# A list of kernel steps for five engines, laid out anew

## The chip, the cores and the metric

The kernel runs on one core of one Trainium2 chip. The metric is the device time of one execution in microseconds (us), the median of several. A profile of one further execution shows when each engine worked. The engines are TensorE (PE in the profile, its weight loads PEld), VectorE (DVE), ScalarE (ACT), GpSimd (POOL) and SyncE (SP), which issues nearly all of the DMA transfers.

## The reference

Two stages. The first is a gated linear attention with a stabilised exponential gate (an mLSTM cell) over 4 batches, 8 heads, 768 tokens and a head size of 40. The second is a feed-forward network (ffn) with a leaky activation whose slope, `alpha`, is given for each hidden unit; it takes all heads of a token as a row of 320.

```python
for t in range(S):
    m_new = np.maximum(f_gate[:, :, t] + m, i_gate[:, :, t])
    f_stab = np.exp(f_gate[:, :, t] + m - m_new)
    i_stab = np.exp(i_gate[:, :, t] - m_new)
    m = m_new
    C = f_stab[:, :, None, None] * C + i_stab[:, :, None, None] * np.einsum('bhd,bhe->bhde', vt, kt)
    n = f_stab[:, :, None] * n + i_stab[:, :, None] * kt
    h_tilde = np.einsum('bhde,bhe->bhd', C, qt)
    nq = np.einsum('bhd,bhd->bh', n, qt)[:, :, None]
    denom = np.maximum(np.abs(nq), 1.0)
    o = 1.0 / (1.0 + np.exp(-o_gate[:, :, t]))
    y[:, :, t] = o * h_tilde / denom
x = y.transpose(0, 2, 1, 3).reshape(B * S, H * D)   # 3072 x 320
h = x @ w_in                                        # w_in 320 x 2048
g = np.maximum(h, 0.0) + alpha * np.minimum(h, 0.0)
out = g @ w_out                                     # w_out 2048 x 320
```

Inputs and output are float32, except `w_in` and `w_out`, which arrive as float64 and are made into float32 on the chip by integer operations.

## The kernel before

**Tiles and stages.** A chunk is 128 tokens of one batch; there are 24. Within a chunk the attention is a product of scores with values under a decay matrix, plus a product with the state left by the chunks before. Two chunks make a group of 256 tokens, and the ffn works on one group at a time: 12 groups, each in 8 steps up (two blocks of 128 hidden units) and 8 steps down. For accuracy each float32 operand of the ffn is split into a high and a low part in a faster format, so that one step up has 16 products of 256 columns and one step down 12 products of 320 columns. The attention of chunks 0 to 5 (`NDIR = 6`) uses plain float32 products; from chunk 6 on it uses parts in bfloat16.

**The list.** The first two groups of the ffn, the attention of chunks 0 to 5, the gates and all loading and splitting of the weights are interleaved by a list written into the kernel, `ORDER` (line 673). Each name in it is a step, and each engine runs its own instructions in the order of the list. Steps that the text names:

- Gates: `sca0`, `sca1` (running maximum over the first 256 tokens and the rest, DVE), `lf..` and `L0`, `L1` (running sum, DVE), `li..`, `bj..`, `wt0`, `wtl` (POOL or DVE), `ewj`, `ewl`, `eeL`, `eel` (exponentials on ACT); `bTt`/`bTc`, `wTt`/`wTc`, `eTt`/`eTc` and `blt`, `wlt`, `elt` turn their rows into columns on PE and copy them out on DVE; `gma gmd gmm gmc` make the decay of the state, `alT`/`alC` turn `alpha`.
- `warmN` (function `warm`): N products of 128x256 in bfloat16 into a buffer that nobody reads.
- A chunk n: `dqn`, `dvn`, `dLn` load q and k, v, and the gate sums; `don` the output gates. `qTn`/`qcn` and `kTn`/`kcn` transpose q and k on PE and copy them on ACT. `spnp` spreads the gate sums over PSUM (a 512-column bar product and four 128-column products), `exnp` takes the exponentials on ACT (four), `scnp` is the scores (four float32 products, eight instructions in the trace), `wgnp` multiplies both on DVE; p is the parity of the head. `vn` is the values (16 instructions of 42 columns), `fmn`/`ftn` the product with the state (8 of 84 columns), `wdn`, `umn`, `ucn` the update of the state, `tan`, `grn`, `ggn`, `gxn`, `gpn` the normalisation, `xn`, `xan`, `xdn` the transposition and splitting of the result for the ffn.
- Weights: `i`, `r` and `o` pieces (columns of `w_in`, its last 64 rows, rows of `w_out`) with `d` load, `s` scale (ACT), either `x` (ACT) and a short join `j`, or `y` and a long join `j` (DVE), `h`, `H` high part (ACT), and the low part, either `l`, `L` on DVE or `p`, `P` on POOL.
- The ffn of groups 0 and 1: `Ugf` or `Vgf` is step up f of group g on PE, followed by `R S G K` or `r s g N`: relu on ACT, combination on DVE, high part on ACT, low part on DVE (`K`) or POOL (`N`). In the U form the activation stays in the PSUM tile `ph` until `K`. `Dgf` is step down f. `Z0`, `Z1` copy a group's result out.

Behind the bar in the list, `A` is one step of the attention from chunk 6 on, which a class `Side` hands out. From the third group on, `Side.until` paces those steps against the ffn by a position, 13 positions a group; a larger starting position means that attention has been taken for further ahead, so that it gets its next steps later.

**The order.** `pin` (line 911) ties the list's instructions together before the scheduler sees them. Every instruction follows the one before it on its engine. In the version before it also follows the last instruction of the list on any engine (`behind`), which orders nothing on the chip but fixes the order in which buffers are handed out. The PSUM buffers of the attention (`psa`, four) are taken by steps in turn.

**The queue.** SP issues the loads in the order of the list, and a load that must wait for its buffer holds up those behind it: q and k have two buffers each, v two.

Of the kernel before, what the change touches and what calls it, by code (L numbers as in the profile page):

```python
# [17 lines left out]
def kernel(ctx: ExitStack, tc: tile.TileContext, q, k, v, i_gate, f_gate, o_gate, w_in, w_out, alpha, out):  # L18
# [7 lines left out]
    GC = 2  # L26
# [582 lines left out]
    def attention(n0):  # L609

        late, x_due = iter(()), []
        for n in range(n0, B * NC):
            if NDIR < n + 1 < B * NC:
                shifted(n + 1)
            loads(n + 2)
            a = iter(())
            far = token_parts(n + 2) if NDIR < n + 2 < B * NC else iter(())
            if n > NBF:
                bb = late_chunk(n, x_due.pop() if x_due else None)
                yield  # L620
# [12 lines left out]
                yield  # L633
                if n + 1 < B * NC:
                    drain(value_parts(n + 1))
                yield
                continue
            bb = stage_b(n)

            order = (a, bb, late, far, a, bb, far) + ((a, bb) if n + 1 < NC else (bb, a))  # L640
            for i, part in enumerate(order):
                next(part, None)
                if i == 5 and n + 2 < B * NC:
                    pre[n + 2] = load_L(n + 2)
                if part in (a, bb):
                    yield
            if NDIR <= n + 1 < B * NC:
                after(n + 1)
            if n % GC == GC - 1:
                late = stage_x(n // GC)  # L650
        for x in x_due:
            p1, p2 = psa(f"p1_{x}"), psa(f"p2_{x}")
            start = len(emitted())
            for j in reversed(range(GC)):
                x_by_channel(x, j, p1, p2, (2, 0, 1))
            block(start, [])
            split_x(x, slice(0, GT), p1, p2)
            yield
# [6 lines left out]
    NDIR = 6  # L665
# [244 lines left out]

    def pin(start):

        last, before = {}, None
        for i in nc.cur_bb.bb.instructions[start:]:
            if before is not None:
                behind(i, before)
            before = i
            if i.engine in last:
                tc.add_manual_dep(
                    i, last[i.engine].name,  # L920
                    mybir.DependencyInfo(mybir.DependencyClass.NoSync, mybir.DependencyReason.DATA), reason="order",
                )
            last[i.engine] = i
        return last
# [10 lines left out]
    def first_group():  # L935
# [417 lines left out]
```

## Time and profile before

| | |
|---|---|
| median of 3 runs | 489.64 us (486.35 to 496.53) |
| the profiled execution | 490.43 us |
| its span, first to last instruction | 488.7 us |
| mean granted TensorE clock | 0.983 |
| DVE, ACT, POOL busy | 62%, 65%, 67% |
| DMA moved | 61.60 MB, mean 126 GB/s |

Matmuls are pipelined, so an instruction's duration is longer than the distance to the next one, and a busy PE is not a PE at its peak. The clock is the share of the full TensorE clock that was granted. A row of a timeline has the start, the time taken, engine, line, operation, tiles and shape, the number of instructions merged, and in brackets the idle time before it with what ended it. In this kernel the list covers the time up to the copy of `Z0`; its part behind the bar and the ten later groups follow.

### The profile page before, as it was taken

Reading aid. Unit: us, or ns where it says so; the run is one execution under the profiler, and the core shown is the slowest. Engines: PE = TensorE matmul, PEld = TensorE weight load, DVE = VectorE, ACT = ScalarE, POOL = GpSimd, SP = SyncE. Lnnn points to the kernel's source line nnn. Section 1 sums busy time; section 2 is a strip of 40 time slices with the busy share of each in tenths; the row PEclk is TensorE's granted clock in tenths of the full one; section 3 lists DMA queues with packets and bytes.
Section 4 is the critical chain, followed back from the end, with each engine's and each line's share of the span. In section 5 each row is a group of like instructions: output and inputs, shape, how many; then the busy total and the mean of one; then the engine's idle time right before and its main releaser. Section 6 shows DMA issues by size and latency. Waiting matters only on the chain.

```text
span 488.7 us, 11761 instructions
## 1 busy us (share of the span) xinstructions
PE 471.9 (97%) x4436; PEld 457.6 (94%) x4436; DVE 303.2 (62%) x647; ACT 317.1 (65%) x706; POOL 327.5 (67%) x410
## 2 busy tenths in 40 slices
PE   8999999999999799999989999999899999999996
PEld 6989889999999799999989989999899999999996
DVE  5848798666854765663873773784683785763221
ACT  4959697886766766675865585675785676343332
POOL 8553467756897698567798399668499595443332
PEclk9959999999999989999999999999999999999999
DMA  9977988968974656579445367588672431000000
GB/s 180 198 205 151 204 213 224 196 129 188 201 178 76 153 116 141 101 179 184 107 108 130 78 142 163 80 167 178 124 172 73 78 93 45 30 1 1 28 1 27
DMA packets 173922, 61.60 MB, mean 126 GB/s; under 512 B 140154, under 2 KB 166122, under 8 KB 173866
## 3 DMA queue, kind: packets, MB, share of 16 engines
q1 hardware_dynamic: 173786, 60.75, 57.0%
q8 instruction: 35, 0.57, 0.5%
q14 instruction: 21, 0.17, 0.1%
q10 hardware_dynamic: 80, 0.11, 0.1%
HBM read 36.90 MB, written 4.03 MB: 84 GB/s over the span
## 4 chain that ended last, share of the span: by engine, by line
PE 70%; DMA 9%; DVE 6%; ACT 6%; POOL 5%; issue 3%; SPq 0%; ACTq 0%; DVEq 0%; POOLq 0%
PE po L750 27%; PE ph L715 4%; PE ph L717 3%; PE ph L716 3%; PE ph L721 3%; PE ph L718 3%; PE ph L720 3%; PE ph L719 3%; PE ph L722 3%; PE pS L1064 2%; DMA qS<-Z 2%; DMA kS<-Z 2%; PE pH L341 2%; DMA wr<-in_moe_w_in_dram 2%; PE pS L437 2%
## 5 line engine op out<-in xcount | busy, mean ns | idle before, releaser
L741 POOL TENSOR_TENSOR gl<-g,gh 128x512 fp32r<-128x512 f32 x89 | 115.0, 1296 | 75.9 <-ACT gh L739 71.6
L730 DVE SCALAR_TENSOR_TENSOR g<-g,oma,ph 128x256 f32<-128x256 f32 x180 | 78.2, 475 | 94.5 <-ACT g L725 88.8
L750 PE MATMUL po<-OH,gh 128*128 128x320 f32 x368 | 111.9, 315 | 0.5 <-ACT gh L739 0.4
L750 PE MATMUL po<-OL,gh 128*128 128x320 f32 x368 | 110.4, 311 | 0.4 <-DVE OL L860 0.4
L725 ACT ACTIVATE g<-ph 128x512 f32<-128x512 f32 x96 | 57.4, 598 | 38.6 <-PE ph L722 27.9
L739 ACT CAST gh<-g 128x512 fp32r<-128x512 f32 x89 | 55.1, 620 | 39.3 <-DVE g L730 38.8
L750 PE MATMUL po<-OH,gl 128*128 128x320 f32 x368 | 70.8, 313 | 0.0
L750 PEld LDWEIGHTS po<-OH,gh 128*128 128x128 f32 x368 | 69.7, 189 | 1.1 <-ACT gh L739 0.8
L750 PEld LDWEIGHTS po<-OL,gh 128*128 128x128 f32 x368 | 69.7, 189 | 0.7 <-DVE OL L860 0.7
L715 PE MATMUL ph<-XH,WH 128*128 128x256 f32 x192 | 55.6, 290 | 7.0 <-DVE g L730 6.5
L412 ACT ACTIVATE E<-Lb,bT 128x128 f32<-128x128 f32 x152 | 47.3, 390 | 16.3 <-PE pH L341 14.1
L750 PEld LDWEIGHTS po<-OH,gl 128*128 128x128 f32 x368 | 57.1, 188 | 0.4 <-POOL gl L741 0.2
L719 PE MATMUL ph<-X,W 128*128 128x256 f32 x192 | 53.8, 280 | 1.0 <-POOL W L860 1.0
L721 PE MATMUL ph<-XL,WH 128*128 128x256 f32 x192 | 54.4, 283 | 0.0
L717 PE MATMUL ph<-XH,WL 128*128 128x256 f32 x192 | 54.4, 283 | 0.0
L720 PE MATMUL ph<-XL,WH 128*128 128x256 f32 x192 | 54.4, 283 | 0.0
L716 PE MATMUL ph<-XH,WH 128*128 128x256 f32 x192 | 54.2, 282 | 0.0
L718 PE MATMUL ph<-XH,WL 128*128 128x256 f32 x192 | 54.2, 282 | 0.0
L722 PE MATMUL ph<-X2L,W 128*128 128x256 f32 x192 | 53.6, 279 | 0.0
L328 ACT CAST E<-pS 128x512 bf16<-128x512 f32 x72 | 41.4, 586 | 7.2 <-DVE pS L326 5.8
L715 PEld LDWEIGHTS ph<-XH,WH 128*128 128x128 f32 x192 | 36.2, 188 | 8.7 <-ACT E L328 6.6
L719 PEld LDWEIGHTS ph<-X,W 128*128 128x128 f32 x192 | 36.6, 191 | 1.2 <-POOL W L860 1.2
(197 smaller groups left out, 1100.2 us busy)
## 6 DMA issues: line engine op xcount, KB each, us to landing
Lb<-L_d SPq DMA_DIRECT2D x20, 512.0 KB
wo<-in_moe_w_out_dram SPq DMA_DIRECT2D x8, 640.0 KB
wi<-in_moe_w_in_dram SPq DMA_DIRECT2D x8, 512.0 KB
qn<-in_q_dram SPq DMA_DIRECT2D x24, 160.0 KB
kn<-in_k_dram SPq DMA_DIRECT2D x24, 160.0 KB
va<-in_v_dram SPq DMA_DIRECT2D x24, 160.0 KB
og<-in_o_gate_dram SPq DMA_DIRECT2D x24, 160.0 KB
out_dram<-ob SPq DMA_DIRECT2D x11, 320.0 KB
```

Of the source, the lines that this page charges most:

```text
L715: nc.tensor.matmul(dst, WH[half][:, 0, hs], XH[:, 0], start=True, stop=False)
L716: nc.tensor.matmul(dst, WH[half][:, 1, hs], XH[:, 1], start=False, stop=False)
L717: nc.tensor.matmul(dst, WL[half][:, 0, hs], XH[:, 0], start=False, stop=False)
L718: nc.tensor.matmul(dst, WL[half][:, 1, hs], XH[:, 1], start=False, stop=False)
L719: nc.tensor.matmul(dst, W2[:, fs], X2, start=False, stop=False)
L720: nc.tensor.matmul(dst, WH[half][:, 0, hs], XL[:, 0], start=False, stop=False)
L721: nc.tensor.matmul(dst, WH[half][:, 1, hs], XL[:, 1], start=False, stop=False)
L722: nc.tensor.matmul(dst, W2[:, fs], X2L, start=False, stop=True)
L725: nc.scalar.activation(gt, ph, AF.Relu, scale=-1.0)
L730: nc.vector.scalar_tensor_tensor(out=y[:, e], in0=gt[:, e], scalar=oma[:, f : f + 1], in1=ph[:, e], op0=ALU.mult, op1=ALU.add)
L741: (nc.vector if split else nc.gpsimd).tensor_tensor(gl, y, gh.bitcast(F32), ALU.subtract)
L750: nc.tensor.matmul(po[j], x[:, e, j * P : (j + 1) * P], W[f // NB][:, f % NB], **ends)
```

## The change

Three edits. `ORDER` is laid out anew up to the bar; behind the bar it is unchanged. The 18 warming products in one step become seven steps of two; several weight pieces and ffn steps change the form in which they are prepared (`x` for `y`, `l` for `p`, `U05` for `V05`, `V10` and `U11` for `U10` and `V11`). `pin` no longer ties instructions across engines. `Side` starts at 26 instead of 25 (1 + 6 x 4). What is computed stays the same.

```diff
@@ -670,23 +670,24 @@
     CP = range(6, 24)
     OBA = range(0)
     FILL = {3: 4, 4: 14, 5: 4}
-    ORDER = """warm18 Cz kfz sca0 lf0a lf0z alT dq0 qT0 qc0 sca1 kT0 lf0b L0 sp00 kc0 r0d r0s sc00 li0 i01d bj0 bTt bTc sc01 wt0 r0y
-        ex00 r0j sp01 ewj wTt wTc eeL ex01 wg01 lf1a lf1b sp11 ex11 li1 dq1 qT1 i00d kT1 alC sp10 wg00 qc1 kc1 dv0 L1
-        bj1 wtl do0 i00s wd0 sc10 i00y i00j um0 uc0 dq2 sc11 wg11 ex10 wg10 lpa eTt eTc lpb v0 gr0 i01s i01x i01j og1
-        fm1 gg0 v1 gma gmd r0h lpc gx0 qT2 kT2 i00h i00p ewl lpd ft1 gp0 dL i20d eel elt i01h qc2 ta1 gr1 kc2 wlt gg1
-        elc gx1 gp1 blt blc wlc x0 x1 i11d i11s i01p lpe gmm gmc sc20 xa0 xd0 i10d xa1 xd1 i10s wd1 sc21 r0p r0H i10x
-        sp20 ex20 sp21 ex21 i11y r0P wg20 wd2 i20s i10j F0 V00 i11j i20x i20j i10h i10p wg21 r00 s00 o0d V01 i11h i21d
-        i11l dq3 qT3 qc3 o0s o0y r01 s01 sp30 ex30 kT3 kc3 dv1 um1 g01 um2 U02 do1 V03 o0j uc1 dv2 uc2 R02 S02 sc30
-        dq4 wg30 g00 i21s i21y o0h sp31 ex31 N00 fm3 ft3 qT4 kT4 i20h r03 i21j o0p sc31 fm2 ft2 s03 G02 i20p qc4 kc4
-        o1d wd4 v2 ta2 dL4 wg31 i21h o1s o1x o1j r2d r2s v3 ta3 o1h o1l wd3 um3 um4 N01 i21l r2x r2j r2h r2p D00 D01
-        uc3 o4d o4s dq6 ex41 o4y gr2 gr3 K02 dL5 og2 gg3 dq5 r2H V04 gx3 V05 uc4 o2d r04 s04 kT5 sc40 wd6 ex40 g03 gg2
-        gx2 r2L gp2 o4j r05 qT5 o2s gp3 qc5 kc5 fm4 sc41 ft4 i30d g04 x2 wg40 dv3 o5d dL7 o2y o2j wg41 i30s i30y x3
-        o4h o4p xa3 N03 s05 ex51 v4 do2 xa2 xd2 ex50 i31d o2h xd3 o2p o5s sc50 um6 uc6 ta4 wg50 F1 U10 o3d D02 o5x
...
-        gx5 R13 S13 D11 o6s o6x o6j o3p N05 G13 D12 x4 gp5 x5 tp0 do3 K13 D13 o6h tp1 tp2 U06 U07 o7s o7y o7j tp3 R06
-        S06 D03 xa5 D04 R07 S07 o7h xa4 xd4 xd5 o6l D05 G06 G07 K06 K07 o7l D06 D07 Z0 | A A V14 r14 s14 g14 N14 A V15
-        r15 s15 g15 N15 A V16 r16 s16 g16 N16 D14 A V17 r17 s17 g17 N17 D15 A A D16 A D17 A Z1 A"""
+    ORDER = """lf0z kfz r0d r0s i10d sca0 lf0a i10s lf0b L0 dq1 alT warm2 warm2 li0 r0y r0j warm2 bj0 i10x sca1 lf1a warm2 sp11 wt0
+        warm2 warm2 dq0 li1 alC bTt bTc ex11 warm2 sp00 qT1 ex00 qc1 sp10 qT0 kT0 sp01 qc0 kc0 sc00 lf1b i10j L1 bj1
+        ewj wTt wTc sc01 wg00 wtl ex01 wg01 dv0 gma Cz i00d i00s i00x wd0 i00j do0 do1 kT1 wd1 eeL dq2 kc1 og1 eel v0
+        sc11 ex10 gr0 gg0 gmd i01d gx0 lpa sc10 um0 dq3 i11d wg10 eTt i10h ewl lpb lpc lpd lpe uc0 eTc elt elc r0h dv1
+        blt blc fm1 wg11 gmm ft1 i10p dL o1d r0H i00h i00p kT2 gmc wlt wlc qT2 qc2 kc2 v1 ta1 i01s o0d i01y sp21 ex21
+        gr1 sp31 um1 uc1 ex31 gg1 sp20 ex20 sc20 i01j i01h gx1 r0L gp0 qT3 qc3 i11s fm2 ft2 gp1 wg20 sc21 i11x x0 x1
+        xa1 og2 wg21 xd1 xa0 xd0 i01p v2 ta2 i11j o1s o1x gr2 i11h kT3 kc3 sp30 ex30 wd2 wd3 F0 um3 um2 uc2 o1j i11l
+        r0p V00 V01 r00 dq4 o0s r01 qT4 qc4 uc3 s00 o0y o0j g00 N00 i20d i20s sc30 wg30 o0h o1h sc31 kT4 kc4 o1p dq5
+        qT5 wd4 wg31 v3 i20y i20j r2d dv2 o0l s01 fm3 dL4 r2s ex41 ft3 sc41 r2y qc5 i21d i21s um4 r2j r2h ta3 r2H i20h
+        gr3 uc4 r2l ex40 U02 gg3 V03 i20l gx3 R02 S02 gp3 wg41 i21x dL5 ex51 D00 kT5 r2L gg2 kc5 r03 i21j i30d i30s
+        i21h sc40 wg40 fm4 ft4 ex50 gx2 gp2 i30y i30j o5d i21l sc50 o4d o4s o5s o5x v4 s03 wg50 g03 g01 ta4 o4y gr4
+        o4j x2 N01 xa2 x3 o5j dq6 xa3 xd3 G02 fm5 do2 K02 dv3 i30h og3 i30p i31d xd2 N03 o4h ft5 o5h o2d V04 r04 s04
+        D01 F1 V10 U11 sc51 o2s o5p o2x o2j gg4 o4l wg51 o3d v5 g04 o3s dq7 gx4 r10 s10 R11 wd6 N04 S11 o3x o2h o2l
...
+        U13 i31s i31x R13 K12 D11 D12 o6j vp1 i31j i31h S13 tp0 i31l G13 U05 o7s K13 do3 D13 tp1 R05 S05 D02 tp2 G05
+        K05 U06 U07 o7y o7j tp3 R06 R07 S07 o6h o6l o7h D03 x4 x5 S06 xa4 xa5 o7l D04 D05 G07 G06 K06 D06 xd5 K07 D07
+        xd4 Z0 | A A V14 r14 s14 g14 N14 A V15 r15 s15 g15 N15 A V16 r16 s16 g16 N16 D14 A V17 r17 s17 g17 N17 D15 A A
+        D16 A D17 A Z1 A"""
...
@@ -910,11 +911,8 @@
 
     def pin(start):
 
-        last, before = {}, None
+        last = {}
         for i in nc.cur_bb.bb.instructions[start:]:
-            if before is not None:
-                behind(i, before)
-            before = i
             if i.engine in last:
                 tc.add_manual_dep(
                     i, last[i.engine].name,
@@ -1295,7 +1293,7 @@
     class Side:
 
         def __init__(self):
-            self.it, self.pos = attention(NDIR), 1 + 6 * (NDIR - GC)
+            self.it, self.pos = attention(NDIR), 26
 
         def step(self):
             self.pos += 1
```

More of the change, by code (lines that the diff above doesn't have):

```diff
@@ L672 @@
     FILL = {3: 4, 4: 14, 5: 4}
-    ORDER = """warm18 Cz kfz sca0 lf0a lf0z alT dq0 qT0 qc0 sca1 kT0 lf0b L0 sp00 kc0 r0d r0s sc00 li0 i01d bj0 bTt bTc sc01 wt0 r0y
-        ex00 r0j sp01 ewj wTt wTc eeL ex01 wg01 lf1a lf1b sp11 ex11 li1 dq1 qT1 i00d kT1 alC sp10 wg00 qc1 kc1 dv0 L1
-        bj1 wtl do0 i00s wd0 sc10 i00y i00j um0 uc0 dq2 sc11 wg11 ex10 wg10 lpa eTt eTc lpb v0 gr0 i01s i01x i01j og1
-        fm1 gg0 v1 gma gmd r0h lpc gx0 qT2 kT2 i00h i00p ewl lpd ft1 gp0 dL i20d eel elt i01h qc2 ta1 gr1 kc2 wlt gg1
-        elc gx1 gp1 blt blc wlc x0 x1 i11d i11s i01p lpe gmm gmc sc20 xa0 xd0 i10d xa1 xd1 i10s wd1 sc21 r0p r0H i10x
-        sp20 ex20 sp21 ex21 i11y r0P wg20 wd2 i20s i10j F0 V00 i11j i20x i20j i10h i10p wg21 r00 s00 o0d V01 i11h i21d
-        i11l dq3 qT3 qc3 o0s o0y r01 s01 sp30 ex30 kT3 kc3 dv1 um1 g01 um2 U02 do1 V03 o0j uc1 dv2 uc2 R02 S02 sc30
-        dq4 wg30 g00 i21s i21y o0h sp31 ex31 N00 fm3 ft3 qT4 kT4 i20h r03 i21j o0p sc31 fm2 ft2 s03 G02 i20p qc4 kc4
-        o1d wd4 v2 ta2 dL4 wg31 i21h o1s o1x o1j r2d r2s v3 ta3 o1h o1l wd3 um3 um4 N01 i21l r2x r2j r2h r2p D00 D01
-        uc3 o4d o4s dq6 ex41 o4y gr2 gr3 K02 dL5 og2 gg3 dq5 r2H V04 gx3 V05 uc4 o2d r04 s04 kT5 sc40 wd6 ex40 g03 gg2
-        gx2 r2L gp2 o4j r05 qT5 o2s gp3 qc5 kc5 fm4 sc41 ft4 i30d g04 x2 wg40 dv3 o5d dL7 o2y o2j wg41 i30s i30y x3
-        o4h o4p xa3 N03 s05 ex51 v4 do2 xa2 xd2 ex50 i31d o2h xd3 o2p o5s sc50 um6 uc6 ta4 wg50 F1 U10 o3d D02 o5x
-        i30j V11 i30h gr4 o5j R10 sc51 S10 dL6 og3 wg51 v5 G10 i30p o6d N04 o5h o5l gg4 gx4 fm5 r11 s11 dq7 o3s vp0
-        K10 D10 g11 N11 g05 ft5 ta5 gr5 i31s i31x i31j o3x i31h gp4 o3j o3h o7d i31l U12 gg5 U13 vp1 R12 S12 G12 K12
-        gx5 R13 S13 D11 o6s o6x o6j o3p N05 G13 D12 x4 gp5 x5 tp0 do3 K13 D13 o6h tp1 tp2 U06 U07 o7s o7y o7j tp3 R06
-        S06 D03 xa5 D04 R07 S07 o7h xa4 xd4 xd5 o6l D05 G06 G07 K06 K07 o7l D06 D07 Z0 | A A V14 r14 s14 g14 N14 A V15
-        r15 s15 g15 N15 A V16 r16 s16 g16 N16 D14 A V17 r17 s17 g17 N17 D15 A A D16 A D17 A Z1 A"""
@@ new lines @@
+    ORDER = """lf0z kfz r0d r0s i10d sca0 lf0a i10s lf0b L0 dq1 alT warm2 warm2 li0 r0y r0j warm2 bj0 i10x sca1 lf1a warm2 sp11 wt0
[11 more added lines that the diff above has]
+        D01 F1 V10 U11 sc51 o2s o5p o2x o2j gg4 o4l wg51 o3d v5 g04 o3s dq7 gx4 r10 s10 R11 wd6 N04 S11 o3x o2h o2l
+        o3j G11 o6d um6 gp4 g10 o6s N10 vp0 U12 dL6 K11 o7d o3h R12 uc6 S12 ta5 gr5 dL7 D10 o3l G12 gg5 gx5 gp5 o6x
+        U13 i31s i31x R13 K12 D11 D12 o6j vp1 i31j i31h S13 tp0 i31l G13 U05 o7s K13 do3 D13 tp1 R05 S05 D02 tp2 G05
+        K05 U06 U07 o7y o7j tp3 R06 R07 S07 o6h o6l o7h D03 x4 x5 S06 xa4 xa5 o7l D04 D05 G07 G06 K06 D06 xd5 K07 D07
+        xd4 Z0 | A A V14 r14 s14 g14 N14 A V15 r15 s15 g15 N15 A V16 r16 s16 g16 N16 D14 A V17 r17 s17 g17 N17 D15 A A
+        D16 A D17 A Z1 A"""
```

## The prediction

> **What bounds the kernel now.** I read the page first, then the busy time by stretches, then TensorE's timeline through the first 36 us, then the timelines of ACT, DVE and the DMA queue in the same place, and last the waits.
>
> ```profile
> span 488.7 us, 11761 instructions
> PE 471.9 (97%) x4436; PEld 457.6 (94%) x4436; DVE 303.2 (62%) x647; ACT 317.1 (65%) x706; POOL 327.5 (67%) x410
> PEclk9959999999999989999999999999999999999999
> ```
>
> TensorE (PE) has work nearly all the time, so a gain has to come from its pace or its few gaps. The third slice of the clock line reads 5: there TensorE ran at half speed. The same by stretches (columns: stretch, length, busy us and instructions of PE, weight loads, DVE, ACT, POOL, then clock, DMA share, GB/s):
>
> ```profile
> 0.00:10.50 10.50, 8.33 (x49) 6.04 (x50) 4.51 (x13) 3.69 (x5) 8.95 (x29) 1.00 0.96 175
> 10.50:22.30 11.80, 11.80 (x107) 10.32 (x105) 9.47 (x19) 10.83 (x31) 6.31 (x6) 1.00 1.04 191
> 22.30:35.90 13.60, 13.60 (x69) 11.74 (x69) 7.39 (x19) 8.11 (x19) 7.84 (x9) 0.50 0.77 213
> 35.90:59.00 23.10, 22.70 (x242) 21.69 (x242) 18.80 (x36) 18.92 (x41) 8.54 (x7) 1.00 0.78 171
> 59.00:104.30 45.30, 43.29 (x356) 42.07 (x355) 37.25 (x75) 37.95 (x81) 33.43 (x39) 1.00 0.87 202
> 161.00:180.00 19.00, 16.27 (x176) 15.42 (x173) 13.84 (x33) 14.04 (x37) 16.64 (x22) 0.91 0.63 138
> ...
> 18.90:22.30 3.40, 3.40 (x32) 3.29 (x30) 3.29 (x10) 3.40 (x9) 1.26 (x3) 1.00 0.68 176
> 25.70:29.10 3.40, 3.40 (x22) 2.98 (x21) 2.17 (x8) 2.43 (x4) 1.03 (x2) 0.50 1.02 381
> ```
>
> The half-clock stretch lasts 13.6 us. What TensorE did ahead of it and in it (start, us, engine, line, what):
>
> ```profile
> 14.05 0.64 PE L232 MATMUL pqk<-ident,qn 128*104 128x128 f32 x4
> 16.36 1.16 PE L1064 MATMUL pS<-qf,kf 104*128 104x128 f32 x8
> 19.14 1.98 PE L305 MATMUL pH<-va,E 128*128 128x42 f32 x16
> 20.95 1.10 PE L359 MATMUL pI<-C,qf 104*128 104x84 f32 x8
> 21.89 3.11 PE L305 MATMUL pH<-va,E 128*128 128x42 f32 x16
> 24.79 1.07 PE L232 MATMUL pqk<-ident,qn 128*104 128x128 f32 x4
> 28.06 1.54 PE L539 MATMUL p<-ident,xn 128*128 128x128 f32 x6
> 30.43 3.78 PE L1064 MATMUL pS<-qf,kf 104*128 104x128 f32 x16
> ```
>
> The clock fell at 22.3 although PE was busy for all of the 3.4 us before (row 18.90:22.30). Those 3.4 us held 16 value products of 42 columns (step v0), 8 state products of 84 (fm1), and the first of the next 16 of 42 (v1). So a queue without gaps does not hold the clock when its products are small. [...]
>
> The list's last product before step Z0 ends at 109.4 us:
>
> ```profile
> 109.44 0.89 DVE L783 COPY ob<-po 128x320 f32<-128x320 f32 x2 [2.83 <-PE po L750]
> ```
>
> From 10.5 to 104.3 us ACT is busy 10.83 + 8.11 + 18.92 + 37.95 = 75.8 of 93.8 us (81%) and DVE 72.9 (78%). Both are close behind PE: an order that frees PE soon meets them.
>
> **The change, part by part.** All terms are against the profiled execution, 490.43 us with a span of 488.7; the median of the runs is 489.64, 0.8 less.
>
> *(a) Clock.* The new list has no two small value steps in a row. v0 is followed by sc11, sc10 and um0, and v1 by sp21, sp31, um1, sp20, sc20. At full clock, the same kinds of work took: 16 value products 1.98 instead of 3.11 (1.13 saved); 8 transposes of q and k 0.64 a four instead of 1.07 (0.86); 16 score products 2 x 1.16 instead of 3.78 (1.46). The other rows of the stretch (6 transposes of x in 1.54, the bars and row sums, 12 transposes of the gates) I scale at the same ratio, about 0.6. They took 13.6 - 3.1 - 2.1 - 3.8 = 4.6 us, so 1.8 is saved, an estimate. Together 5.3. Ends: 5.3 if the clock never falls and nothing else holds PE, 0 if it falls as before. I take 4.3: the kinds are mixed, but elt, blt, fm1, gmm, kT2, wlt, qT2 still stand together ahead of v1.
>
> *(b) Waits of PE behind the weights.*
>
> ```profile
> L719 PE MATMUL ph<-X,W 128*128 128x256 f32 x192 | 53.8, 280 | 1.0 <-POOL W L860 1.0
> L750 PE MATMUL po<-OL,gh 128*128 128x320 f32 x368 | 110.4, 311 | 0.4 <-DVE OL L860 0.4
> 63.58 0.39 PE L715 MATMUL ph<-XH,WH 128*128 128x256 f32 x1 [0.42 <-DVE gl L741]
> ```
>
> V04 waited for the low part of the rest rows (r2p on POOL), D01 for o1l, V05 for K02, which frees its ph. In the new list r2d is issued ahead of dv2 and r2l stands ahead of U02, some 70 steps before V04; o1p comes soon behind V00, long before D01. So 1.0 + 0.4 = 1.4 is saved. K02 now stands twelve steps ahead of V04, so the third, 0.4, I leave as it is: it is what is late next.
>
> *(c) The start.* The two weight pieces r0d and i10d (each 128 x 512 x 8 bytes = 512 KB; a q or k of a chunk has 128 x 320 x 4 = 160 KB) go ahead of q and k, and chunk 1 goes ahead of chunk 0.
>
> ```profile
> 1.27 0.42 SPq L99 DMA_DIRECT2D qn<-in_q_dram  x1
> 2.36 1.64 SPq L814 DMA_DIRECT2D wr<-in_moe_w_in_dram  x2
> ...
> 8.71 0.67 ACT L824 ACTIVATE t_wr<-wr 128x512 f32<-128x512 f32 x1 [0.35 <-DMA wr<-in_moe_w_in_dram]
> 10.53 1.14 ACT L1047 ACTIVATE E<-pb,bT 128x128 f32<-128x128 f32 x4 [1.16 <-DVE bT L993]
> ...
> 4.27 0.68 DVE L1111 TENSOR_TENSOR_SCAN g_WL<-g_WH 32x256 f32<-32x256 f32 x1 [2.31 <-DMA g_WH<-in_i_gate_dram]
> 5.33 1.27 DVE L1111 TENSOR_TENSOR_SCAN g_WL<-g_WH,g_WL 32x512 f32<-32x512 f32 x1
> 8.16 0.41 DVE L1185 TENSOR_TENSOR g_WH<-g_li,g_L 32x256 f32<-32x256 f32 x1 [0.47 <-POOL g_li L1182]
> 10.86 1.46 DVE L848 SCALAR_TENSOR_TENSOR t_wr<-wr,t_wr 128x512 uint32<-128x512 uint32 x1
> ```
>
> At the 175 GB/s of row 0.00:10.50, 1024 KB of weights and 320 KB of chunk 1 take 7.7 us, so q of chunk 0, until now the second load of all, comes at about 13 us (behind the gates at 4.2). That is hidden: the first exp (10.53) waits for bT, not for q, and meanwhile PE has the seven warm steps, sp11, bTt and sp00, which need only gates. If that cover went, it would cost up to 7.7. The path to the first exp is L0, bj0, bTt, bTc on DVE and PE. sca1 (1.27) leaves it ahead of L0, r0y and r0j come onto it ahead of bj0 and wait for r0s. r0 lands at about 4.2 + 512 / 175 = 7 us (8.7 before), then 0.67 + 0.4 + 1.46, so bj0 starts near 9.6 instead of 8.16, and sca1 then holds bTc to about 11.3. First exp about 11.6: +1.1. The 14 warming products instead of 18 cost nothing and save nothing, since PE waits for L0 behind them.
>
> *(d) More work for DVE and ACT.* Counting the letters of both lists: low parts on POOL 12 to 7, on DVE 8 to 13; the ACT preparation of a piece (x) 9 to 10; the undivided ffn form (U, subtraction on DVE) 6 to 7. DVE gets six more such subtractions:
>
> ```profile
> 58.01 0.68 DVE L860 TENSOR_TENSOR WL<-t_wi,WH 128x512 fp32r<-128x512 f32 x1
> ```
>
> 6 x 0.68 = 4.1 us, less one shift and the longer join that goes with it (about 0.8, half the 1.46 of r0j above), 3.3 us, so its share from 10.5 to 104.3 goes from 78% to 81%. ACT gets 0.7. Ahead of V00 ACT now also has ex30, ex31 (1.14 each by the row of 10.53), qc3, kc3, og2, i00x, i11x, o1s and o1x, and no longer i01x and i20s. Ends: 0, as ACT had 35.9 - 3.69 - 10.83 - 8.11 = 13.3 us idle there, and +3.3, all of DVE's addition. I take a quarter, +0.8.
>
> *(e) The queue of loads.* dq3 and dv2 blocked the queue behind wd1 and um1:
>
> ```profile
> 21.70 0.69 SPq L99 DMA_DIRECT2D qn<-in_q_dram  x1
> 31.10 0.38 SPq L99 DMA_DIRECT2D kn<-in_k_dram  x1
> 35.48 6.56 SPq L112 DMA_DIRECT2D va<-in_v_dram  x2
> ```
>
> Between 22.4 and 31.1 nothing was issued behind dq3. In the new list wd1 stands right behind kT1, um1 behind v1, so the pieces come sooner; what waits for them (V00, D00) is already in (a) and (b), so 0.
>
> *(f) pin without the order across engines.* Each engine's own order stays. What may change is which PSUM or SBUF buffer a step gets, thus a wait for a buffer like the 0.42 at 63.58 above. Ends -0.4 and +0.4, I take 0: no step of PE loses or gains an operand.
>
> *(g) Side starts at 26 instead of 25:* from the third group on, attention stands one step later against the ffn. Where this shows today:
>
> ```profile
> PE ph L715 <- DVE g L730: 6.5, 6, 2.3
> 171.03 0.35 PE L715 MATMUL ph<-XH,WH 128*128 128x256 f32 x1 [2.33 <-DVE g L730]
> ```
>
> Six waits, 6.5 us, and after the longest one the clock drops (row 161.00:180.00: 0.91 of 19 us, 1.7 us lost). Ends: -8.2, all gone; +16.8, every one of ten groups with the longest wait (10 x 2.33 - 6.5). Which DVE work meets which ffn step changes for all groups; the rows show no side, so 0.
>
> **Sum.** -4.3 - 1.4 + 1.1 + 0.8 = -3.8: 486.6 as profiled, 485.8 as a median.
>
> **Rivals.** *A, the clock falls again.* Row 25.70:29.10 speaks for it: PE was busy for all 3.40 us, with nothing but transposes (from the end of those at 24.79 to those at 28.06), and the clock stayed at 0.50. The new list puts 20 transposes (elt, blt, kT2, wlt, qT2) around fm1 and gmm ahead of v1, and PE will wait there for ACT and DVE as well. Then (a) is 0 and the sum +0.5: 490.9 profiled, 490.1 as a median. [...] *B, more than forecast.* (a) in full, (d) at 0, (b) with the other gaps of rows 35.90:59.00 and 59.00:104.30 (0.4 + 2.0), and the wait at 171 with its half clock gone: -5.3 - 2.4 + 1.1 - 2.3 - 1.7 = -10.6: 479.8, or 479.0 as a median. For it: the gaps it takes are all waits, not work; against it: (c), and four gains at once. *C, slower.* Attention one step later puts a DVE step ahead of the ffn's g in every group. At 2.33 each, +16.8 - 3.8 = +13.0: 503.4, or 502.6. It decides from 13.6 us on (485.8 to 499.4), 1.4 more a group than today's 0.65. Against it: today's six waits differ (6.5 / 6 = 1.1 on average, 2.3 the longest), so one place in the cycle of steps is bad and others are not.
>
> **How the numbers follow.** Forecast 0.57, A 0.22, B 0.14, C 0.07. The forecast's own range is 481 to 488.5. The range 478.5 to 491.5 adds A and most of B and leaves out C and the far end of B. Two per cent (9.8 us) is about what a measurement of this kernel can tell from no change. Faster by more: most of B, 0.11. Slower by more: C, 0.06. Within: 0.83.
>
> **What would show it.** (a) the clock at 1.00 from 20 to 36 us and v1's 16 products in about 2 us; (b) no PE wait for W; (c) first exp near 11.6; the first ph product near 39 us, but with fm2, sc21, v2 and um3 done ahead of it; (d) the copy of Z0 near 105; (g) the L715 waits. Wrong if Z0 comes before 101 or after 109, or if what follows Z0 differs from 379 us by over 4.

## The result, and the profile after

The changed kernel takes 503.4 us (median of 4 executions, 502.91 to 507.08) where the kernel before took 488.0 in the same measurement. The ratio is 1.0344, 95% interval 1.0265 to 1.0422: slower, where 485.8 us and no measurable change were forecast. Executions of one kernel spread by up to 4%: times in this text are medians of all of them, and the ratios leave out those that took over 1.5% more than the fastest of their kernel.

The page of the profiled execution (502.91 us), and its busy time by stretches, columns as before:

```profile
span 501.2 us, 11751 instructions
PE 482.5 (96%) x4432; PEld 466.3 (93%) x4432; DVE 304.5 (61%) x652; ACT 317.2 (63%) x707; POOL 319.5 (64%) x404
PEclk9996998999999999999999999999999999999999
```

```profile
0.00:10.50 10.50, 5.79 (x24) 3.83 (x24) 4.63 (x13) 3.08 (x4) 5.66 (x24) 1.00 0.94 173
10.20:26.30 16.10, 16.10 (x65) 13.10 (x66) 5.54 (x8) 7.43 (x21) 8.34 (x10) 1.00 0.71 113
37.10:47.30 10.20, 10.20 (x65) 9.01 (x66) 4.45 (x13) 6.24 (x17) 0.32 (x1) 0.50 0.41 141
53.40:122.90 69.50, 66.44 (x545) 65.31 (x540) 56.26 (x107) 56.46 (x119) 36.79 (x42) 0.98 0.79 188
122.90:501.20 378.30, 367.65 (x3591) 359.77 (x3590) 222.78 (x485) 231.62 (x521) 259.99 (x318) 1.00 0.51 108
```

What follows Z0 takes 378.3 us (before 488.7 - 109.4 = 379.3). So the whole loss lies in the list: Z0's copy came at 109.44 and comes at 122.91, 13.5 us later. Within it the first ph product comes at 53.4 instead of 35.7 (17.8 later), and from there to Z0 the new list needs 69.5 us instead of 73.8 (4.3 less, since it does more ahead of that product: 545 products are left, 632 in before).

The row 10.20:26.30 holds the riddle: PE is busy for all of 16.10 us and runs only 65 products, where before had 107 in 11.8. TensorE's timeline through the start shows why:

```profile
4.05 0.26 PE L1128 MATMUL pa<-ident,al 16*128 16x16 f32 x1 [4.05 <-DMA al<-in_moe_alpha_dram]
4.24 1.89 PE L145 MATMUL warm<-ident 128*128 128x256 bf16 x8
5.93 0.63 PE L93 MATMUL pb<-later,ident 128*128 128x512 bf16 x1
6.49 2.07 PE L1017 MATMUL pb<-g_L,ident 32*128 32x128 f32 x8
8.49 1.03 PE L145 MATMUL warm<-ident 128*128 128x256 bf16 x4
10.18 0.42 PE L987 MATMUL ps_gb<-ident,g_WH 32*128 32x32 f32 x2 [0.66 <-DVE g_WH L1183]
11.50 2.07 PE L1017 MATMUL pb<-g_L,ident 32*128 32x128 f32 x8
13.50 1.09 PE L232 MATMUL pqk<-ident,qn 128*104 128x128 f32 x4
19.26 2.07 PE L1017 MATMUL pb<-g_L,ident 32*128 32x128 f32 x8
21.26 2.08 PE L1062 MATMUL pS<-qf,kf 104*128 104x128 f32 x8
```

Every product takes nearly twice its time of before: four transposes of q 1.09 (0.64), eight scores 2.08 (1.16). The eight spread instructions of an `sp` step, which follow its 512-column bar, serve below as a clock meter: together 1.15 us at full clock, 2.07 at half. The same eight in before:

```profile
7.75 1.15 PE L1019 MATMUL pb<-g_L,ident 32*128 32x128 f32 x8 [0.41 <-DVE g_L L1120]
11.47 1.15 PE L1019 MATMUL pb<-g_L,ident 32*128 32x128 f32 x8
```

So TensorE runs at half clock from the start. The clock column reads 1.00 there and is wrong: until the clock's first recorded change, here at 33.7 us, it shows full speed, whatever the products say. In before, TensorE worked at half clock from its first product at 1.4 us to 5.3 (the 18 warming products took 4.01 us there, where 26 take 3.01 at full clock in e10 below) and from 22.3 to 36, some 17.5 us. Here it did so from 4.1 to 33.7, from 37.1 to 47.3, and for 3.4 us behind the one long wait between V00 and Z0 (81.08 below, where before had none), some 43 us:

```profile
81.08 0.55 PE L539 MATMUL p<-ident,xn 128*128 128x128 f32 x3 [1.50 <-ACT XH L558]
81.50:84.90 3.40, 3.40 (x19) 3.40 (x18) 3.40 (x7) 3.35 (x7) 2.78 (x3) 0.50 0.67 184
```

About 26 us more of half clock, at half a microsecond lost for each while PE has work (the 0.50 of the rows), is an estimate of 13 us, the size of the loss. That is arithmetic, not proof; the order of the steps could hold the start by itself.

The changes of the clock that the two traces record come 3.41 us or a whole multiple of it apart: at 5.3, 22.4, 36.0, 172.6 and 176.0 us in before, at 33.7, 37.1, 47.4, 81.5 and 84.9 in `after`. Some expectations below call such a step a window.

### The profile page after: what moved, and what is told of

The parts are those of the page before. It is cut to its first block, busy times and chain, and to the rows that moved or that the text cites. A ratio compares the mean times of both kernels' runs of the same rounds, so it can differ in the third digit from the quotient of the medians.

```text
span 501.2 us, 11751 instructions
## 1 busy us (share of the span) xinstructions
PE 482.5 (96%) x4432; PEld 466.3 (93%) x4432; DVE 304.5 (61%) x652; ACT 317.2 (63%) x707; POOL 319.5 (64%) x404
## 4 chain that ended last, share of the span: by engine, by line
PE 70%; DVE 8%; ACT 6%; DMA 6%; POOL 5%; issue 4%; SPq 0%; ACTq 0%; DVEq 0%; POOLq 0%
PE po L751 28%; PE ph L716 4%; PE ph L718 3%; PE ph L719 3%; PE ph L717 3%; PE ph L721 3%; PE ph L722 3%; PE ph L720 3%; PE ph L723 3%; PE pH L341 3%; DMA qS<-Z 2%; PE pS L437 2%; DVE g L731 2%; PE pS L1062 2%; POOL gl L742 1%
## 5 line engine op out<-in xcount | busy, mean ns | idle before, releaser
L723 PEld LDWEIGHTS ph<-X2L,W 128*128 128x128 f32 x192 | 36.8, 192 | 0.0
```

The costliest lines, as they stand in the source:

```text
L723: nc.tensor.matmul(dst, W2[:, fs], X2L, start=False, stop=True)
```

## The experiments

Theory W: the new list loses TensorE's clock, and that is the loss. Rivals: D, the dependences of the new order (gates, loads, ScalarE) hold the start at whatever clock; Q, q and k of the chunks come late; P, the lost order across engines in `pin` moves buffers; G, the shift of `Side`. All runs in one table: median time, ratio to the kernel before run beside it, the time of the eight products of the first four `sp` steps (the clock meter), start of the first ph product, and Z0's copy, in us. The last three columns are from the profiled execution; those of e5 and e13 (marked *) took 494.94 and 501.73 us, 8 and 14 us more than their medians.

| run | time | ratio, 95% interval | sp steps | ph | Z0 |
|---|---|---|---|---|---|
| before | | | 1.15 1.15 1.15 1.15 | 35.7 | 109.4 |
| after | 503.4 | 1.034, 1.027 to 1.042 | 2.07 2.07 2.07 2.07 | 53.4 | 122.9 |
| e1, after | 502.1 | 1.032, 1.028 to 1.037 | 1.15 2.07 2.07 2.07 | 52.9 | 122.2 |
| e2, before | 489.8 | 1.004, 1.001 to 1.007 | 1.15 1.15 1.15 1.15 | 35.6 | 107.4 |
| e3, after | 509.3 | 1.046, 1.042 to 1.051 | 2.07 2.07 2.07 2.07 | 58.6 | 127.7 |
| e4, after | 502.4 | 1.033, 1.028 to 1.037 | 2.07 2.07 2.07 2.07 | 51.9 | 120.4 |
| e5, before | 486.6 | 1.001, 0.997 to 1.005 | 1.15 1.15 1.15 2.07 * | 41.8 * | 115.0 * |
| e6, before | 486.6 | 0.997, 0.993 to 1.001 | 1.15 1.15 1.15 1.15 | 31.4 | 105.0 |
| e7, after | 496.0 | 1.017, 1.009 to 1.024 | 1.15 2.07 2.07 1.22 | 49.0 | 118.7 |
| e8, before | 500.6 | 1.025, 1.017 to 1.034 | 2.07 2.07 2.07 2.07 | 48.0 | 119.8 |
| e9, after | 492.1 | 1.013, 1.008 to 1.019 | 1.15 1.15 1.15 1.15 | 43.1 | 114.6 |
| e10, after | 490.2 | 1.008, 1.004 to 1.011 | 1.15 1.15 1.15 1.15 | 43.1 | 113.9 |
| e11, after | 490.2 | 1.008, 1.005 to 1.012 | 1.15 1.15 1.15 1.15 | 42.9 | 112.5 |
| e12, before | 501.3 | 1.027, 1.020 to 1.035 | 2.07 2.07 2.07 2.07 | 50.6 | 122.3 |
| e13, before | 487.3 | 1.002, 0.999 to 1.005 | 1.15 2.07 2.07 2.07 * | 48.5 * | 121.2 * |
| e14, after | 489.5 | 1.006, 1.003 to 1.009 | 1.15 1.15 1.15 1.15 | 40.1 | 111.1 |
| e15, after | 502.1 | 1.034, 1.029 to 1.038 | 1.15 1.15 2.07 2.07 | 52.5 | 121.6 |
| e16, after | 501.4 | 1.025, 1.015 to 1.034 | 1.15 1.15 2.07 2.07 | 52.7 | 121.9 |
| e17, after | 496.9 | 1.019, 1.006 to 1.033 | 1.15 2.07 2.07 2.07 | 47.9 | 117.5 |
| e18, after | 495.6 | 1.014, 1.009 to 1.019 | 1.15 1.15 1.15 1.15 | 39.3 | 109.8 |

"after" or "before" is the list that the run starts from. The diffs show words of the list that change, with a neighbour or two.

**The warming products.** e1 puts the 18 back at the head of the new list; e2 cuts those of the old list up as the new one does.

```diff
 # e1, in after (and without the seven warm2)
-lf0z kfz r0d
+warm18 lf0z kfz r0d
 # e2, in before
-warm18 Cz kfz
+Cz kfz
-alT dq0
+alT warm2 warm2 warm2 warm2 dq0
-sp00 kc0
+sp00 warm2 warm2 kc0
-bTt bTc
+bTt warm2 bTc
```

> The new kernel with one step warm18 ahead of its list and none of the seven warm2; nothing else moved. Theory W (TensorE never left half clock before 33.7 us, because the warming products now come in pieces of 8, 4 and 2 with small 32-row products between): the clock is full from about 5 us, the spread products take about 1.1 instead of 2.07 us, the copy of Z0 comes at 108 to 113 us instead of 122.9, and the time is 488 to 493 us. Rival Q (q and k come too late, behind two weight pieces): the clock may rise, but Z0 stays at 119 or later and the time at 499 or more. Rival P (buffers handed out in another order since pin was cut): as Q, no change beyond 2 us.

> The kernel before with its warm18 cut into the same pieces as in the new list (8 behind alT, 4 behind sp00, 2 behind bTt); nothing else moved. Theory W: the start stays at half clock, v0's 16 products take about 3.4 us, Z0 comes at 115 to 123 instead of 109.4, and the time is 494 to 502 us. Rivals Q and P: no change, 486 to 490 us.

The 18 raise the clock (first `sp` 1.15), but it falls again behind a wait of 2.73 us, and the time stays at 1.032. TensorE in e1:

```profile
6.15 1.15 PE L1017 MATMUL pb<-g_L,ident 32*128 32x128 f32 x8
10.04 0.42 PE L987 MATMUL ps_gb<-ident,g_WH 32*128 32x32 f32 x2 [2.73 <-DVE g_WH L1183]
10.93 2.07 PE L1017 MATMUL pb<-g_L,ident 32*128 32x128 f32 x8
```

Cut up in the old list they cost 0.4%. Both times miss what W gave (488 to 493 and 494 to 502). So fewer and later warming products alone are not the cause.

**Late q and k, and `pin`.** e3 issues chunk 1 and 0 ahead of the weights; e4 takes back the edit of `pin`; e5 takes the old list with the new `pin` and `Side`.

```diff
 # e3, in after
-kfz r0d r0s i10d
+kfz dq1 dq0 r0d r0s i10d
 # e4, in after
-        last = {}
+        last, before = {}, None
...
+            if before is not None:
+                behind(i, before)
+            before = i
 # e5, in before
-            self.it, self.pos = attention(NDIR), 1 + 6 * (NDIR - GC)
+            self.it, self.pos = attention(NDIR), 26
```

> The new kernel with the loads of q and k of chunks 1 and 0 moved ahead of the weight pieces r0 and i10; nothing else moved. Rival Q: first scores earlier by 5 us or more and 495 to 499 us. Theory W: TensorE is still busy at half clock, q is not what it waits for, so within 2 us of the new kernel, 501 to 505 us. Rival P: no change either.

> The new list and Side at 26, but pin with its order across engines as before. Rival P: most of the loss goes, 488 to 495 us. Theory W and rival Q: within 2 us of the new kernel, 501 to 505 us, with half clock up to 33 us.

> The list of before with the two other edits of the change: pin without the order across engines, and Side from 26. Theory W (the new list keeps TensorE at half clock for nearly all of its first 47 us, and that is the loss) and the theory that the list's order holds it by its dependences both expect the time of before: 485 to 490 us, Z0's copy at 108 to 111, what follows it 378 to 380 us. Theory G (the shift of Side costs a wait of DVE in every group) expects 494 to 503 us, with all of the addition behind Z0. Theory P (pin's lost order moves buffers) expects more than 3 us more ahead of Z0.

Q falls: earlier q and k make it slower, 1.046, where W gave no change, since the weight piece r0 then comes later and VectorE's r0y, ahead of the gate step bj0, waits 5.50 us for it (timeline of DVE in e3):

```profile
11.94 0.43 DVE L841 TENSOR_SCALAR t_wr<-t_wr 128x512 uint32<-128x512 uint32 x1 [5.50 <-ACT t_wr L825]
```

P falls with e4, and P and G with e5, whose time is that of before. The list is left.

**Clock or dependences.** e6 puts six dense products ahead of the value products of v0 and of v1 in the old list; e7 puts 18 at the head of the new list and four behind each of 15 steps; e8 takes all 18 from the old list; e13 is e6 again, in more executions.

```diff
 # e6, e13, in before
-    FILL = {3: 4, 4: 14, 5: 4}
+    FILL = {0: 6, 1: 6, 3: 4, 4: 14, 5: 4}
 # e7, in after with warm18 at the head: behind sp11 bTt sp00 sp10 kT0 sp01 wTt kT1 v0 um0 blt gmm wlt v1 um1
+warm4
 # e8, in before
-warm18 Cz kfz
+Cz kfz
```

> The kernel before with six dense warming products between the pieces of steps v0 and v1 each (about 1 us of TensorE each at full clock), to hold the clock through 22 to 36 us. Theory W: the half clock of 22.3 to 36 us goes or becomes shorter, the first ph product comes at 31 to 33 us instead of 35.7, Z0's copy at 104 to 107, 482 to 486 us. The theory that dependences, not the clock, set the start: the first ph product stays within 1 us of 35.7 and Z0 within 2 us of 109, 486 to 490 us.

> The kernel after with 18 warming products at the head of the list and four dense ones behind each of 15 of its small steps (sp11, bTt, sp00, sp10, kT0, sp01, wTt, kT1, v0, um0, blt, gmm, wlt, v1, um1): about 4 us more of TensorE's work ahead of the first ph product at full clock. Theory W: the clock stays full from about 6 us on, v0 comes at 17 to 20 us instead of 26.3, the first ph product at 38 to 44 instead of 53.4, Z0's copy at 107 to 114 instead of 122.9, and the time is 487 to 494 us. The theory that the new order's dependences (gates, loads, ACT) hold the start whatever the clock is: Z0 at 118 or later, 499 us or more.

> The kernel before without its 18 warming products. Theory W: the clock first rises only where dense products stand together, v0 comes at 22 to 27 us instead of 19.1, the first ph product at 38 to 46 instead of 35.7, and the time is 490 to 500 us. The theory that the start is held by dependences: the first ph product within 1 us of 35.7 and 486 to 490 us.

> The kernel of e6 again, in more rounds. If term (a) of the prediction holds in the median as in the profiled execution: a ratio of 0.990 to 0.996 with an interval below 1, 483 to 485 us. If most executions of the kernel before lose less to the half clock than the profiled one did: a ratio of 0.996 to 1.001.

e8 makes the loss in the old list: started cold, with nothing else changed, it takes 1.025 and its first ph product comes 12.3 us later, somewhat more than W gave. D has no reason for that. e6 does in its trace what term (a) of the prediction hoped for: 1.00 through the former half-clock stretch, Z0 4.4 earlier. Between medians nothing is left of it, 0.997 and in e13 1.002: the execution of before that was profiled seems to have lost more to the clock than most (490.43 us against medians of 487, a mean granted clock of 0.983 where most others read 0.985 to 0.993), and the 12 products cost time too. e7 is between the theories: the clock fell in a wait behind `sp11` and came back at 22.6 us. TensorE in e7:

```profile
7.37 0.61 PE L145 MATMUL warm<-ident 128*128 128x256 bf16 x4
10.53 0.42 PE L987 MATMUL ps_gb<-ident,g_WH 32*128 32x32 f32 x2 [2.55 <-DVE g_WH L1183]
12.27 2.07 PE L1017 MATMUL pb<-g_L,ident 32*128 32x128 f32 x8
```

That wait of 2.55 us for the gates, which `after` has too but fills in part at half clock, became the suspect.

**The gap.** e10 fills it with 26 dense products and adds nothing later; e9 adds e7's fillers, e11 those of e6; e15 fills half of it. e12 is the mirror: a gap of the same kind made in the old list.

```diff
 # e10, e15 (13), in after with warm18 at the head
-sp11 wt0
+sp11 warm26 wt0
 # e12, in before
-alT dq0 qT0 qc0 sca1 kT0 lf0b L0 sp00 kc0 r0d r0s sc00 li0 i01d bj0 bTt bTc sc01
+alT dq0 sca1 lf0b L0 r0d r0s li0 i01d bj0 bTt bTc qT0 qc0 kT0 sp00 kc0 sc00 sc01
```

> The kernel of e7 with 26 instead of 4 dense products behind sp11, to fill the 2.55 us in which TensorE waited for the gates there. Theory W (the clock, and only it): the clock stays full from about 5.5 us to the first ph product, which comes at 41 to 44 us instead of 49.0; Z0's copy at 110 to 114, and 487 to 491 us; what stays above before is the 15 fillers. Theory that the order's dependences hold the start: the first ph product within 2 us of 49.0, and 494 to 498 us.

> The kernel after with 18 warming products at the head of the list and 26 dense ones behind sp11, where TensorE waits for the gates, and no filler after that. If that one gap lost the clock (theory W, gap): full clock from about 5.5 us on to at least 20, v0 at 18 to 21 us instead of 26.3, the first ph product at 37 to 46, 486 to 496 us. If the kinds of the new order cannot hold it (theory W, kinds): the clock falls one or two windows behind the filler, by 16 us, the first ph product at 47 to 52 and 496 to 502 us. Dependences alone: 500 us or more.

> As the run with the gap filled alone, and with six dense products each ahead of the value products of v0 and v1 (1.3 us of TensorE at full clock in all). Theory W, gap: the clock stays full to the first ph product, which comes at 36 to 40 us, Z0's copy at 104 to 110 and 482 to 488 us. Theory W, kinds: as the run without these fillers, within 2 us.

> The mirror: the list of before with the steps of the gates (L0, li0, bj0, bTt, bTc) moved ahead of qT0, kT0, sp00 and sc00, so that TensorE waits about 3 us for the gates at 5.6 to 8.6 us and has the same work behind it. Theory W, gap: the clock falls one window behind its first rise, by 9 to 12 us, and comes back only at 30 to 40 us; the first ph product at 42 to 48 us instead of 35.7, 494 to 502 us. Dependences alone: no more than the gap itself, the first ph product at 36 to 39, 487 to 493 us.

> As e10 with 13 dense products in the gap behind sp11 instead of 26, so that some 1.2 us of it stay. If any gap of that size loses the clock: as with no filler (e1), the clock falls by 10 us and stays low to 30 or later, first ph product at 49 to 53 us, 498 to 502 us. If the clock needs only most of a window filled: as e10, first ph product at 42 to 44, 488 to 492 us.

This decides for W from both sides. 26 products that nobody reads bring the new list from 1.032 (e1) to 1.008, 502.1 to 490.2 us. A wait of 2.97 us brings the old one to 1.027, with the same work behind it; its first ph product, at 50.6, is later still than expected. TensorE in e10, then in e12:

```profile
7.33 3.01 PE L145 MATMUL warm<-ident 128*128 128x256 bf16 x26
10.27 0.31 PE L987 MATMUL ps_gb<-ident,g_WH 32*128 32x32 f32 x2
10.83 1.15 PE L1017 MATMUL pb<-g_L,ident 32*128 32x128 f32 x8
```

```profile
8.57 0.35 PE L989 MATMUL ps_gb<-ident,g_WH 32*128 32x32 f32 x2 [2.97 <-DVE g_WH L1185]
11.83 2.07 PE L1019 MATMUL pb<-g_L,ident 32*128 32x128 f32 x8
13.83 3.78 PE L1064 MATMUL pS<-qf,kf 104*128 104x128 f32 x16
```

Half the filler buys nothing (e15: 1.034): 2.06 us of wait remain, the clock holds to 12.4 us (9.3 in e1) and falls. e9's more fillers cost more than they bring, and its time missed what W had given (487 to 491). e11's are worth nothing in the median: not the 482 to 488 us of the first theory, but e10's time, as the second had it.

The half clock comes in steps of 3.4 us in the experiments too: 10.2 us of it in e10 (25.8 to 36.0), 20.5 in e15 (12.4 to 32.9). But the wait that lost the clock was shorter than a step, 2.97 us (e12) and 2.06 us (e15), and `after` was busy for 16.10 us, more than four steps, without gaining it.

**What is left, and what makes the gap.** e14 is e10 with four dense products behind um0, blt, gmm and wlt. e16 leaves out all fillers and moves the two weight steps r0y and r0j from ahead of the gates to behind them; e17 adds e14's four fillers, e18 to that eight products behind sp11 and sp00 each.

```diff
 # e16, in after with warm18 at the head
-li0 r0y r0j bj0
+li0 bj0
-bTt bTc ex11 sp00
+bTt bTc r0y r0j ex11 sp00
 # e18, in e17
-sp11 wt0
+sp11 warm8 wt0
-sp00 qT1
+sp00 warm8 qT1
```

> As the run with the gap filled alone (e10), and four dense products each behind um0, blt, gmm and wlt (1.8 us at full clock in all), where the clock fell at 25.8 us for 10.2 us. If that fall is the rest of the loss: no half clock between 6 and 45 us, the first ph product at 39 to 41 us instead of 43.1, Z0's copy at 109 to 112, 486 to 489 us. If not: 490 us or more.

> The kernel of e1 (18 warming products at the head of the new list) with r0y and r0j moved from ahead of bj0 to behind bTc, and no filler. If those two steps on VectorE make the gap that loses the clock: bTt at 7.3 to 7.8 us instead of 10.2, no wait of TensorE over 0.6 us ahead of 11 us, full clock from about 5.5 us to at least 19, the first ph product at 38 to 44 us, 485 to 492 us. If loads or ScalarE make another gap behind it: the first ph product at 49 or later and 498 us or more.

> As the run with r0y and r0j behind the gates, and four dense products each behind um0, blt, gmm and wlt. If the clock then holds from 5.5 us to the first ph product: that product at 36 to 39 us, Z0's copy at 105 to 109, 483 to 488 us. If not: the same as without them, within 2 us.

> The kernel of e17 (r0y and r0j behind the gates, four dense products each behind um0, blt, gmm and wlt) with eight dense products behind sp11 and eight behind sp00 (0.9 us each at full clock). If windows of 32-row spreads do not hold the clock and dense products do: full clock from 5.5 us to the first ph product, that product at 36.5 to 40 us instead of 47.9, Z0's copy at 106 to 111, 484 to 489 us, no slower than before by 0.5%. If the waits behind bTt lose it: the clock falls by 13 us, the first ph product at 44 or later, 493 us or more.

e14 holds the clock to the first ph product, at 40.1, and gives back 122.9 - 111.1 = 11.8 of the 13.5 us; its median, 489.5, is just beyond what was expected. e16 was to show that r0y and r0j make the gap. They do: bTt comes at 7.16, and of PE's waits 0.84 and 0.64 us are left. And yet the clock falls, and the time, 501.4 us, is that of e1 (e17, where the clock comes back at 31.5 us, 1.019). So without that gap the loss is still there: the first theory of e16 fails, and the second has the time right, but the waits that it rests on are short. The stretch in which it is lost is busier than one that holds it. First e16, then before:

```profile
5.90:9.30 3.40, 2.97 (x20) 2.22 (x19) 1.94 (x6) 2.02 (x3) 1.68 (x3) 1.00 1.23 210
9.30:12.70 3.40, 2.35 (x8) 1.59 (x9) 3.12 (x3) 3.40 (x11) 3.40 (x4) 0.50 1.51 138
```

```profile
5.30:8.70 3.40, 2.67 (x19) 1.96 (x18) 2.71 (x6) 1.75 (x3) 2.73 (x6) 1.00 1.01 236
8.70:12.10 3.40, 3.40 (x26) 2.80 (x26) 1.80 (x3) 2.24 (x7) 3.32 (x4) 1.00 1.27 219
```

2.97 us of e16's stretch are busy, most of them with the 32-row spreads of sp11 and sp00. In before 2.67 are, with eight transposes of 128 rows beside one step of spreads, and the clock holds. So the gap is one way to lose it. That an order of kinds without large products is another is argued from these rows; what decided in e16 stays open. e18 puts dense products among the spreads, and its trace does as W expected: all four `sp` steps at 1.15, ph at 39.3, Z0 at 109.8, 490.39 us in that execution. But the median is 495.6 (489.78 to 504.38): other executions of the same program go otherwise, as they do of the kernel before (484.36 to 498.41 beside it). No version beat the kernel before.

**The old order can lose it too.** The traces of e5 and e13, which have the start of the old list, are of such executions. TensorE in e13:

```profile
8.25 1.15 PE L1019 MATMUL pb<-g_L,ident 32*128 32x128 f32 x8 [0.56 <-DVE g_L L1120]
9.34 1.16 PE L1064 MATMUL pS<-qf,kf 104*128 104x128 f32 x8
10.66 2.07 PE L1064 MATMUL pS<-qf,kf 104*128 104x128 f32 x8
13.09 2.07 PE L1019 MATMUL pb<-g_L,ident 32*128 32x128 f32 x8
```

No wait of PE from 2 to 16 us is longer than 0.56 us there, and yet the clock falls at 10.7 us and stays low to 48.2, as in the new list. In e5 it falls at 13.8, without a wait of PE. In these two it had first risen at 7.3 and 7.0 us, in before and e6, where it held to 22 us or longer, at 5.3 and 4.5. In the traces of lists that begin with 18 warming products the first rise comes anywhere from 4.1 to 7.3 us. So the steps of 3.4 us do not stand at one place against the start of the kernel. That their place decides what the old order loses is argued from these four traces, not tried. Of the 94 executions of the kernel before beside these runs 14 took 497 us or more, of `after`, e1, e15 and e16 all 16 did. So, by the times, the new order loses the clock in each execution, the old one now and then.

## Why the prediction was wrong

- **(c) is the step that failed**, in its last sentence: "The 14 warming products instead of 18 cost nothing and save nothing, since PE waits for L0 behind them." It counted those waits as cover that makes other things free, and put the cut of the warming products at nothing. With the 18 products back and the wait filled (e10) 13.2 us of the median come back (503.4 to 490.2): hardly any with the products alone (e1, 1.3), 11.9 more with the wait filled. In the old list the products are worth 13 us (e8). The rest of (c) came out: the first exp is at 11.55 (11.6 forecast), and no wait of PE is put down to q or k. The 11.6 owes something to luck: r0j took 0.69 us, not 1.46, and a table load of 1.28 us on ScalarE, which the sum did not have, made up for it. In before it ran at 1.73 us, out of the way; in `after` r0s is ScalarE's first step, and the load waits with it for the weights:

```profile
6.66 1.28 ACT L825 ACT_TABLE_LOAD   x1 [6.66 <-DMA wr<-in_moe_w_in_dram]
7.95 0.67 ACT L825 ACTIVATE t_wr<-wr 128x512 f32<-128x512 f32 x1
```

  r0y and r0j were priced at +1.1 as a delay of the exps. They also open the gap on PE, but since e16 is as slow without it, how much of the loss is theirs stays open.
- **(a) had the mechanism right and the bounds wrong.** It treated the clock as a stretch that goes or stays, ends 5.3 and 0, and rival A did the same with 490.1. Neither asked whether the clock rises in the new start at all, though the prediction's own row for the old v0 and v1 showed that a full queue can lose it. That small products make it do so was read from that one row and no run shows it alone: e6 held the clock with 12 dense products among them, and e13, the same kernel, lost it at 10.7 us among scores and spreads. The end on the wrong side is what e8 and e12 cost the old list: 13 and 14 us between medians. Its size for the old stretch, 4.3, was met in e6's trace (4.4), not between medians.
- **(b)** was right: nothing waits for W or OL any more.

```profile
L751 PE MATMUL po<-OL,gh 128*128 128x320 f32 x368 | 109.5, 309 | 0.0
L720 PE MATMUL ph<-X,W 128*128 128x256 f32 x192 | 53.6, 279 | 0.0
```

- **(e), (f)** at 0 stand: no wait of PE for q, k or a weight piece shows in the start of `after`, nor at full clock in that of e10, and e4 changes nothing outside its interval.
- **(g)** at 0 stands: e5, and 378.3 against 379.3 us behind Z0. The waits of ph for g fell from 6.5 to 3.1 us, and others came:

```profile
PE ph L716 <- DVE g L731: 3.1, 4, 1.7
PE po L751 <- POOL gl L742: 1.7, 1, 1.7
PE po L751 <- ACT gh L740: 1.3, 2, 1.2
```

- **(d)** (+0.8) is not told apart by any run. The wait of 1.50 us at 81.08, for ScalarE, and the 3.4 us at half clock behind it may be of its kind: 1.5 + 1.7 = 3.2 us. e14 has the same wait, and 6.8 us at half clock behind it: 1.5 + 3.4 = 4.9 us, more than the 1.7 us by which its Z0 is later than in before. That ScalarE's added work makes this wait is argued, not tried.
- **Rival C** named the time, 502.6, and not the cause: nothing was lost in the groups behind Z0.

In numbers: the first ph product came 17.8 us late. With the clock held it comes at 40.1 (e14), so about 13.3 of that is clock; the other 4.5 comes back as the 4.3 us less up to Z0.

## What to carry to other kernels

Price the start of an order by what TensorE's clock does in each stretch of some 3.4 us (its recorded changes come in steps of 3.41 here), with durations of equal products as the meter: a wait of 2 to 3 us in the first 11 us cost 12 to 14 us here (e1 against e10, e12 against before), since the half clock then stayed on through a queue without gaps. A wait on TensorE is no free cover for moving work, and the 18 warming products at the head were of use here only where no long wait came behind them. Before believing a gain of 1% from the clock, look at many executions: one trace of e6, e13 or e18 would have misled.

## What the runs showed of the hardware

- The clock column of a profile read 1.00 until the first recorded change (33.7 us in `after`), also where products take 1.8 times their full-speed time (2.07 against 1.15).
- Eight dense warming products in a row (1.89 us) did not raise the clock in `after`, where a bar and spreads followed; in e2 the same eight did (the first `sp` step at 1.15), with transposes of q and k behind them, and e7's clock rose at 22.6 us behind 3.4 us that were about half dense products and half transposes. So transposes among dense products did not keep it from rising, where alone, in the row 25.70:29.10 of rival A, it stayed at 0.50. 18 products (up to 4.0 us) raised it in each trace that had them at the head, at 4.1 to 7.3 us.
- The price of the gap was a step, not a slope: filled 490.2, half filled 502.1, unfilled 502.1 us (e10, e15, e1).
- At half clock TensorE can be busy without a gap and stay there: 34.10 of 34.10 us in e16.

```profile
12.70:46.80 34.10, 34.10 (x185) 30.15 (x184) 14.09 (x34) 18.52 (x46) 9.54 (x14) 0.50 0.66 146
```
